# A matmul over 64 rows of the array, done over all 128 rows with zeros

## The chip, the cores and the metric

The kernel runs on one core of one Trainium2 chip. The metric is the device time of one execution in microseconds. A time given for a kernel is the median of several runs.

The core has five engines that the profile names: PE (TensorE, matmuls; PEld is its loading of weights, which overlaps), DVE (VectorE), ACT (ScalarE), POOL (GpSimd) and SP (SyncE, which issues the transfers). Each executes its own instructions in order. They wait for each other at semaphores.

## The reference

Two stages follow each other: an attention of eight batches and eight heads with a feature map, and a feed-forward layer on its output ("MoE" in the code's names, with one expert).

```python
def phi(x):                               # x: batch, head, 576 tokens, 64
    proj = x @ w_phi                      # 64 -> 128 features
    proj = proj - max(abs(proj), last axis)
    return concat([exp(proj), exp(-proj)])  # 256 features
q_p, k_p = phi(q), phi(k)
kv  = einsum('bhsf,bhsd->bhfd', k_p, v)
z   = sum of k_p over tokens
out = (q_p @ kv) / (q_p @ z + 1e-6)

h = x @ w_in                              # 4608 tokens, 512 -> 2048
y = max(0.01 * h, h) @ w_out              # 2048 -> 512
```

The change is in the product of `k_p` and `v`.

## The kernel before

**Numbers.** Most matmuls run on float32r operands. A factor that needs more precision is split into a high part (the value rounded to float32r) and a remainder (value minus high part). A product is then three matmuls: high by high, remainder by high, high by remainder, all added up in the same PSUM tile. In the attention, `vh` and `vl` are the high part and remainder of the values, `kph` and `kpl` those of the features of the keys. `vh` has two extra columns of ones, so that the sum `z` comes out of the same matmul, and so it has 66 columns where `vl` has 64.

**Work.** The attention goes over 32 pairs of heads (4 pairs by 8 batches). For each pair there is a key phase (`k_phase`) and a query phase (`q_phase`). The first eight pairs run their key phase on plain float32, without the split (the branch `nat`, and `first_k_phase` for the first four); the other 24 use the split. The feed-forward layer goes over 18 blocks of 256 tokens and 16 groups of 128 hidden units: `layer1` (lines 542, 543 and 545 issue its matmuls, ACT applies the activation, and the result is split into `gh` and `gl`) and, three steps later, `layer2` (lines 562 to 564).

**A key phase.** A pair of heads has 576 tokens, taken in chunks of 128 on the partitions. Four chunks (c = 0 to 3) hold the first 512 tokens. For each chunk and head (j = 0, 1) the two-part features meet the two-part values in three matmuls over 128 rows. The fifth chunk (c = 4) holds tokens 448 to 575, of which only the last 64 are new. They lie on partitions 64 to 127 (the slice `r`). Their high part goes to the upper half of the tile `kst` by a cast on DVE (recorded at line 69), and their remainder to its lower half, partitions 0 to 63, by a subtraction on DVE (line 264). `kst` appears as `kph` in the profile, after the buffer that it shares. The values of these tokens are loaded twice, into both halves of columns 8 and 9 of `rv`, so `vh[:, 8 + j]` holds them in both halves. One matmul over 128 rows then gives high by high and high by remainder together. What is left is remainder of values by high part of features: a matmul over the 64 upper rows alone, `vl[r, 8 + j]` by `kst[r, j]`. The helper `kv_mm` issues all of these, so they have line 206. In 24 key phases there are 48 of the 64-row matmuls. `vl` is one tile for the whole program, written for each pair by POOL (recorded at line 72); columns 8 and 9 of it are written and read on partitions 64 to 127 alone.

**Order.** The work is written as generators. A key phase and a query phase advance in turn, attention is advanced beside the feed-forward steps, and priorities are given. A scheduler with a model of the engines' time then fixes each engine's order before the program runs. So an edit in one place can move instructions in many. On the chip each engine follows this order.

Of the kernel before, what the change touches and what calls it, by code (L numbers as in the profile page):

```python
# [9 lines left out]
F32 = mybir.dt.float32  # L10
# [34 lines left out]
def attention_moe_kernel(ctx: ExitStack, tc: tile.TileContext, q, k, v, vt, w_phi, w_in, w_out, out):  # L45
    nc = tc.nc
# [4 lines left out]
    def ct(shape, dt, name):  # L51
        return cp.tile(shape, dt, tag=name, name=name)

    def st(shape, dt, tag):
        return sp.tile(shape, dt, tag=tag, name=tag, bufs=BUFS.get(tag, 1))
# [8 lines left out]
    def copy_(key, o, i):  # L64
        e = pick(key) or "a"
        if e == "a":
            nc.scalar.copy(o, i)  # L67
        else:
            (nc.vector if e == "v" else nc.gpsimd).tensor_copy(o, i)  # L69

    def tt_(key, o, a, b, op):
        (nc.vector if pick(key) == "v" else nc.gpsimd).tensor_tensor(o, a, b, op=op)  # L72

    def pt(tag):
        return ps.tile([P, 512], F32, tag=tag, name=tag, bufs=PBUFS[tag])
# [19 lines left out]
    vh = ct([P, 10, 66], F32R, "vh")  # L95
    vl = ct([P, 10, 64], F32R, "vl")
    nc.gpsimd.memset(vh[:, :, 64:66].bitcast(F32), 1.0)

    f1, f2, f3, f4 = (cp.tile([P, 2048], F32, tag="late", name=n, bufs=4) for n in ("f1", "f2", "f3", "f4"))
    fk = [None, f2, f1, f4]  # L100
# [87 lines left out]
    def k_phase(i):  # L188
# [16 lines left out]
        def kv_mm(j, lt, rt, first=False, last=False):  # L205
            nc.tensor.matmul(kvp[0 : lt.shape[1], 256 * j : 256 * j + 256], lhsT=lt, rhs=rt,  # L206
                             start=first and j == 0, stop=last, skip_group_check=True)

        for g in range(3):
            w = 2 if g < 2 else 1  # L210
            r = slice(0, P) if g < 2 else slice(64, P)
            n = P if g < 2 else 64
            m4 = st([P, 4], F32, "m4")
            pmk = st([P, 4, F], F32, "pmk")
            if nat:
                pk = pt("a")
                for s in range(w):
                    t0 = (2 * g + s) * P if g < 2 else S - P
                    proj(pk, s, rk[:, t0 : t0 + P])
                pkv = pk[r, 0 : 256 * w].rearrange("p (a f) -> p a f", f=F)  # L220
            else:
                for s in range(w):
                    t0 = (2 * g + s) * P if g < 2 else S - P
                    pk = pt("a")
                    for j in range(2):
                        nc.tensor.matmul(pk[:, 256 * j : 256 * j + 256], lhsT=ks[:, j, t0 : t0 + P],
                                         rhs=wq.rearrange("p a f -> p (a f)"), start=True, stop=True)
                    pk = pk[r].rearrange("p (j x f) -> p j x f", j=2, x=2)
                    x = pmk[r, 2 * s : 2 * s + 2]
                    copy_("pk", x, pk[:, :, 1])  # L230
                    nc.vector.tensor_tensor(x, pk[:, :, 0], x, op=ALU.add)
                    yield
                pkv = pmk[r, 0 : 2 * w]
            nc.vector.tensor_reduce(m4[r, 0 : 2 * w], pkv, axis=AX.X, op=ALU.max, apply_absolute_value=True)
            mb = m4[r, 0 : 2 * w].unsqueeze(2).broadcast_to([n, 2 * w, F])
            if nat:
                nc.vector.tensor_tensor(pmk[r, 0 : 2 * w], pkv, mb, op=ALU.subtract)
            else:
                tt_("ksub", pkv, pkv, mb, ALU.subtract)
            yield  # L240
            for s in range(w):
                c = 2 * g + s
                ek = st([P, 2, 256], F32, ("ek", "kph", "kpl")[c % 3] if nat else "ek")
                nc.scalar.activation(ek[r, :, 0:F], pmk[r, 2 * s : 2 * s + 2], AF.Exp)  # L244
                nc.scalar.activation(ek[r, :, F:256], pmk[r, 2 * s : 2 * s + 2], AF.Exp, scale=-1.0)
                if nat:
                    for j in range(2):
                        kv_mm(j, rv[r, 4 * j + c if c < 4 else 8 + j], ek[r, j], first=c == 0, last=c == 4)
                    yield
                    continue  # L250
                if c < 4:
                    kph = st([P, 2, 256], F32R, "kph")
                    kpl = st([P, 2, 256], F32R, "kpl")
                    copy_("kph", kph, ek)
                    tt_("kpl", kpl, ek, kph.bitcast(F32), ALU.subtract)
                    for j in range(2):
                        kv_mm(j, vh[:, 4 * j + c], kph[:, j], first=c == 0)
                        kv_mm(j, vl[:, 4 * j + c], kph[:, j])
                    for j in range(2):
                        kv_mm(j, vh[:, 4 * j + c], kpl[:, j])  # L260
                else:
                    kst = st([P, 2, 256], F32R, "kph")
                    copy_("kst", kst[r], ek[r])
                    nc.vector.tensor_tensor(kst[0:64], ek[r], kst[r].bitcast(F32), op=ALU.subtract)
                    for j in range(2):
                        kv_mm(j, vl[r, 8 + j], kst[r, j])
                        kv_mm(j, vh[:, 8 + j], kst[:, j], last=True)
                yield
        kvs = st([P, 2, 256], F32, "ek").rearrange("p a (b f) -> p a b f", b=2)[0:66]
# [107 lines left out]
    def proj(pk, s, x):  # L377
        nc.tensor.matmul(pk[:, 256 * s : 256 * s + 256], lhsT=x, rhs=bd, start=True, stop=True)
# [132 lines left out]
    def attention():  # L511
        for i in range(NP, B * NP + 1):
            gens = [k_phase(i)] if i < B * NP else []
            if i > NP:
                gens.append(q_phase(i - 1))
            while gens:
                for it in list(gens):
                    if next(it, end) is end:
                        gens.remove(it)
                    else:  # L520
                        yield i - 1
            yield i
# [127 lines left out]
```

## Time and profile before

| | |
|---|---|
| median of 3 runs | 1243.11 us (1240.61 to 1243.74) |
| the profiled execution, whole | 1238.5 us |
| its span, first to last instruction | 1236.7 us |
| PE busy in the span | 1187.8 us, 96% |
| DVE busy | 854.6 us, 69% |
| ACT busy | 797.0 us, 64% |
| POOL busy | 669.4 us, 54% |
| TensorE clock granted, mean | 0.994 of full speed |

The profile is of one execution. "PE busy" is the time in which at least one matmul is under way. Matmuls overlap: the next may start well before the last one's recorded end. A group of instructions is shown by line, engine, operation and tile as `out<-in`. Forms such as `64*64 64x256` stand for rows and columns of weights, then partitions and elements of the moving operand. After the bar come busy time and mean duration of one, then idle time of the engine before them and what ended it. Split key phases run from about 230 us to 1045 us; what follows is feed-forward work alone.

### The profile page before, as it was taken

What the parts mean: (1) busy time and instruction counts of PE and PEld (TensorE: products, weight loads), DVE (VectorE), ACT (ScalarE), POOL (GpSimd) and SP (SyncE); (2) the same over time, 40 slices, a digit from 0 to 9 for tenths busy, and PEclk for the clock granted to TensorE, in tenths of its full rate; (3) what the DMA queues carried; (4) which work ended last, traced back from release to release, by engine and by line L of the source; (5) the groups of instructions that cost most, each with busy time, mean ns of one, the idle gap of its engine ahead of it and who ended that gap; (6) DMA issues with size and microseconds to landing.
All of it is one profiled execution on the core that took longest, in us unless ns stands there. A gap on an engine that the chain in (4) does not pass through costs nothing. (4 is left out here: it accounts for less than half of the span.)

```text
span 1236.7 us, 21143 instructions
## 1 busy us (share of the span) xinstructions
PE 1187.8 (96%) x7496; PEld 1035.8 (84%) x7496; DVE 854.6 (69%) x1357; ACT 797.0 (64%) x2027; POOL 669.4 (54%) x701
## 2 busy tenths in 40 slices
PE   8898799999999999999899999999999999999998
PEld 5686577779888989889798988989888888999997
DVE  6999854698888888888888898806887788200000
ACT  5987765677777777777677777736766766433232
POOL 0132122467767676767667777836666767433232
PEclk9999899999999999999999999999999999999999
DMA  7345411011111111111111111100111100000000
GB/s 209 116 135 160 147 47 41 10 54 34 39 30 48 31 35 44 31 48 31 30 38 39 31 48 31 39 20 28 31 48 31 29 20 1 19 17 1 18 18 17
DMA packets 62777, 57.00 MB, mean 46 GB/s; under 512 B 45136, under 2 KB 46288, under 8 KB 62672
## 3 DMA queue, kind: packets, MB, share of 16 engines
q1 hardware_dynamic: 62672, 55.65, 15.8%
q8 instruction: 59, 0.97, 0.3%
q14 instruction: 46, 0.38, 0.1%
HBM read 46.20 MB, written 9.44 MB: 45 GB/s over the span
## 5 line engine op out<-in xcount | busy, mean ns | idle before, releaser
L72 POOL TENSOR_TENSOR gl<-g,gh 128x256 fp32r<-128x256 f32 x288 | 241.9, 842 | 294.8 <-ACT gh L67 237.1
L542 PE MATMUL h<-xh,w0h 128*128 128x256 f32 x1152 | 299.1, 286 | 4.5 <-ACT g L549 1.8
L543 PE MATMUL h<-xh,w0l 128*128 128x256 f32 x1152 | 298.2, 285 | 0.4 <-DVE w0l L72 0.4
L562 PE MATMUL acc<-w1h,gh 128*128 128x512 f32 x576 | 231.0, 401 | 10.4 <-ACT gh L67 8.3
L542 PEld LDWEIGHTS h<-xh,w0h 128*128 128x128 f32 x1152 | 218.4, 190 | 21.2 <-ACT g L549 2.7
L543 PEld LDWEIGHTS h<-xh,w0l 128*128 128x128 f32 x1152 | 218.2, 189 | 14.3 <-issue 1.9
L563 PE MATMUL acc<-w1l,gh 128*128 128x512 f32 x576 | 228.5, 397 | 0.0
L564 PE MATMUL acc<-w1h,gl 128*128 128x512 f32 x576 | 220.3, 398 | 0.0
L545 PE MATMUL h<-xl,w0h 128*128 128x256 f32 x1152 | 206.3, 284 | 0.0
L549 ACT ACTIVATE g<-h 128x256 f32<-128x256 f32 x288 | 109.2, 382 | 133.3 <-PE h L545 93.6
L72 POOL TENSOR_TENSOR ql<-eq,qh 128x576 fp32r<-128x576 f32 x96 | 159.5, 1668 | 38.7 <-DVE qh L69 26.3
L545 PEld LDWEIGHTS h<-xl,w0h 128*128 128x128 f32 x1152 | 167.2, 190 | 2.1 <-issue 0.4
L67 ACT CAST gh<-g 128x256 fp32r<-128x256 f32 x288 | 114.3, 402 | 75.5 <-PE acc L563 72.3
L562 PEld LDWEIGHTS acc<-w1h,gh 128*128 128x128 f32 x576 | 109.0, 189 | 26.3 <-ACT gh L67 10.5
L72 POOL TENSOR_TENSOR kpl<-ek,kph 128x512 fp32r<-128x512 f32 x72 | 101.9, 1415 | 49.9 <-PE c L206 22.1
L69 DVE CAST qh<-eq 128x576 fp32r<-128x576 f32 x96 | 99.2, 1037 | 35.5 <-ACT eq L344 20.1
L564 PEld LDWEIGHTS acc<-w1h,gl 128*128 128x128 f32 x576 | 106.6, 189 | 19.5 <-POOL gl L72 0.5
L563 PEld LDWEIGHTS acc<-w1l,gh 128*128 128x128 f32 x576 | 109.1, 189 | 12.4
L69 DVE COPY o<-acc 128x512 f32<-128x512 f32 x17 | 11.7, 687 | 130.4 <-DMA out_dram<-o 129.5
L72 POOL TENSOR_TENSOR ring<-ring,mb 128x576 f32<-128x576 f32 (+1 forms) x37 | 47.9, 1293 | 88.2 <-DVE mb L500 42.9
L343 ACT ACTIVATE eq<-mb 128x288 f32<-128x288 f32 x112 | 49.3, 440 | 67.8 <-DVE mb L338 60.4
L244 ACT ACTIVATE ek<-pmk 128x256 f32<-128x256 f32 (+1 forms) x128 | 53.4, 417 | 58.6 <-POOL pmk L72 21.0
(176 smaller groups left out, 2412.3 us busy)
## 6 DMA issues: line engine op xcount, KB each, us to landing
out_dram<-o SPq DMA_DIRECT2D x35, 256.0 KB, 2.0
ring<-in_w_in_dram SPq DMA_DIRECT2D x16, 512.0 KB, 3.7
ring<-in_w_out_dram SPq DMA_DIRECT2D x16, 512.0 KB, 3.6
rk<-in_k_dram SPq DMA_DIRECT2D x27, 288.0 KB, 2.8
rq<-in_q_dram SPq DMA_DIRECT2D x26, 288.0 KB, 2.8
rv<-in_v_dram SPq DMA_DIRECT2D x29, 256.0 KB, 3.4
rv<-in_vt_dram SPq DMA_DIRECT2D x58, 32.0 KB, 2.9
f<-in_k_dram SPq DMA_DIRECT2D x3, 288.0 KB, 3.3
```

The costliest lines, as they stand in the source:

```text
L67: nc.scalar.copy(o, i)
L69: (nc.vector if e == "v" else nc.gpsimd).tensor_copy(o, i)
L72: (nc.vector if pick(key) == "v" else nc.gpsimd).tensor_tensor(o, a, b, op=op)
L244: nc.scalar.activation(ek[r, :, 0:F], pmk[r, 2 * s : 2 * s + 2], AF.Exp)
L343: nc.scalar.activation(eq[:, 0], mb[:, u], AF.Exp)
L542: nc.tensor.matmul(ph, lhsT=weight(0, "h", ft)[:, d * P : d * P + P], rhs=xh[:, d], start=d == 0, stop=False)
L543: nc.tensor.matmul(ph, lhsT=weight(0, "l", ft)[:, d * P : d * P + P], rhs=xh[:, d], start=False, stop=False)
L545: nc.tensor.matmul(ph, lhsT=weight(0, "h", ft)[:, d * P : d * P + P], rhs=xl[:, d], start=False, stop=d == NP - 1)
L549: nc.scalar.activation(g, ph, AF.Prelu, alpha=0.01)
L562: nc.tensor.matmul(a, lhsT=gh[:, ts], rhs=weight(1, "h", ft), start=ft == 0, stop=False)
L563: nc.tensor.matmul(a, lhsT=gh[:, ts], rhs=weight(1, "l", ft), start=False, stop=False)
L564: nc.tensor.matmul(a, lhsT=gl[:, ts], rhs=weight(1, "h", ft), start=False, stop=ft == NFT - 1)
```

## The change

The matmul of the values' remainders for the last 64 tokens now takes all 128 rows of both operands. The lower half of its left operand, `vl[0:64, 8:10]`, is set to zero once at the start by POOL, so the product is the same: the lower rows add zero times the features' remainders. The moving operand is now the whole of `kst[:, j]`, both halves.

```diff
     vh = ct([P, 10, 66], F32R, "vh")
     vl = ct([P, 10, 64], F32R, "vl")
     nc.gpsimd.memset(vh[:, :, 64:66].bitcast(F32), 1.0)
+    nc.gpsimd.memset(vl[0:64, 8:10].bitcast(F32), 0.0)
...
                     copy_("kst", kst[r], ek[r])
                     nc.vector.tensor_tensor(kst[0:64], ek[r], kst[r].bitcast(F32), op=ALU.subtract)
                     for j in range(2):
-                        kv_mm(j, vl[r, 8 + j], kst[r, j])
+                        kv_mm(j, vl[:, 8 + j], kst[:, j])
                         kv_mm(j, vh[:, 8 + j], kst[:, j], last=True)
```

All line numbers above 97 are one higher in the changed kernel, so its line 207 is line 206 of before.

The scheduler's order changes with it. On PE, in the first split key phase, at the matmuls of the last 64 tokens (`kph` is the tile `kst`; `qs` and `wq` belong to a query phase, `ks` to the next pair's keys), before:

```order
L226 MATMUL a<-wq,ks 128x256 [waits DVE_49]
L206 MATMUL c<-kph,vl 64x256 [waits DVE_49]
L319 MATMUL a<-qs,wq 128x288 [waits PE_49,Activation_49]
L320 MATMUL a<-qs,wq 128x288
L206 MATMUL c<-kph,vh 66x256 [waits DVE_49]
L206 MATMUL c<-kph,vl 64x256
L206 MATMUL c<-kph,vh 66x256
```

and now:

```order
L227 MATMUL a<-wq,ks 128x256 [waits DVE_49]
L320 MATMUL a<-qs,wq 128x288 [waits PE_49,Activation_49]
L321 MATMUL a<-qs,wq 128x288
L207 MATMUL c<-kph,vl 64x256 [waits DVE_49]
L207 MATMUL c<-kph,vh 66x256
L207 MATMUL c<-kph,vl 64x256
L207 MATMUL c<-kph,vh 66x256
```

The size behind the tiles is that of the output, so the 64 there is columns of `vl` in both. The first `vl` matmul has moved behind the query's two, next to its `vh`, and one wait for DVE stands where two stood.

The same place on PE in the second split key phase, where the work between is layer 1's, before:

```order
L543 MATMUL h<-xh,w0l_798 128x256
L206 MATMUL c<-kph,vl 64x256 [waits DVE_49]
L542 MATMUL h<-xh,w0h_797 128x256
L543 MATMUL h<-xh,w0l_798 128x256
L542 MATMUL h<-xh,w0h_797 128x256
L543 MATMUL h<-xh,w0l_798 128x256
L542 MATMUL h<-xh,w0h_797 128x256
L206 MATMUL c<-kph,vh 66x256 [waits DVE_49]
L206 MATMUL c<-kph,vl 64x256
L206 MATMUL c<-kph,vh 66x256
```

and now:

```order
L543 MATMUL h<-xh,w0h_798 128x256
L544 MATMUL h<-xh,w0l_799 128x256
L543 MATMUL h<-xh,w0h_798 128x256
L544 MATMUL h<-xh,w0l_799 128x256
L207 MATMUL c<-kph,vl 64x256 [waits DVE_49]
L207 MATMUL c<-kph,vh 66x256
L207 MATMUL c<-kph,vl 64x256
L207 MATMUL c<-kph,vh 66x256
```

The first `vl` matmul stands six places later, behind more of layer 1, and the four are together.

On POOL, at the start of the program, now:

```order
L128 MEMSET bd 128x256
L125 MEMSET rv 128x10x2
L125 MEMSET f_79 128x10x2
masks.py:197 MEMSET ident 128x128
L97 MEMSET vh 128x10x2
L98 MEMSET vl 64x128
masks.py:199 ISA
masks.py:199 AFFINE_SELECT ident<-ident 128x128
```

The new memset of `vl` stands behind those of `bd`, which holds `w_phi`, and of the first tiles; the other rows stand as before.

## The prediction

> **What bounds the kernel now.** I read the page's engine table and slices first, then a table by stage, then the groups by form, the timeline around the changed matmul, the waits, and last the chain.
>
> ```profile
> span 1236.7 us, 21143 instructions
> PE 1187.8 (96%) x7496; PEld 1035.8 (84%) x7496; DVE 854.6 (69%) x1357; ACT 797.0 (64%) x2027; POOL 669.4 (54%) x701
> PE   8898799999999999999899999999999999999998
> DVE  6999854698888888888888898806887788200000
> PEclk9999899999999999999999999999999999999999
> ```
>
> TensorE is busy nearly all the time, at nearly full clock, so the clock is no term of the sum. DVE stands at 8 to 9 tenths while attention runs and is the second limit there. The stage table (stretch, length, then busy time and count of PE, PEld, DVE, ACT, POOL) gives the margin in the stage where the changed matmuls lie, and in a piece of it that the chain below covers.
>
> ```profile
> 230.00:1050.00 820.00, 797.72 (x5277) 712.56 (x5275) 669.16 (x1015) 573.89 (x1495) 559.64 (x546) 1.00 0.12 34
> 971.00:1045.00 74.00, 71.19 (x470) 62.72 (x469) 60.04 (x92) 53.17 (x141) 52.84 (x54) 1.00 0.06 17
> ```
>
> TensorE is idle for 820 - 797.72 = 22.3 us there (2.7%), and for 74 - 71.19 = 2.8 us (3.8%) in the piece. DVE is busy 669.16 of 820, or 82%. So the stage runs at the pace of TensorE, with some points at which TensorE has to wait.
>
> But a busy TensorE need not be a TensorE at its peak. Overlapped matmuls count as busy even where they are spaced out. What a matmul costs the stream is the time from its start to the next one's start. The groups by form hint at it:
>
> ```profile
> L206 PE MATMUL c<-kph,vl 128*64 128x256 f32 x192 | 49.5, 280 | 0.0
> L206 PE MATMUL c<-kph,vl 64*64 64x256 f32 x48 | 15.7, 328 | 0.7 <-DVE kph L69 0.7
> L206 PEld LDWEIGHTS c<-kph,vl 64*64 64x64 f32 x48 | 6.2, 129 | 10.4 <-issue 5.4 <-DVE kph L69 1.6 <-DVE kph L264 0.6
> ```
>
> The first row is the same product on 128 rows (of the first 512 tokens), the second the 64-row form that the change replaces: 48 of them, two in each of 24 phases. They are only 48 ns longer each, which alone would be 2.3 us. The third row tells more: the weight loads of this form have 10.4 us of idle time before them, most of it "issue", that is, waiting for nothing that the profile shows.
>
> **The timeline shows the real price.** First the normal case, the 128-row form between its neighbours (start, duration):
>
> ```profile
> 229.85 0.28 PE L206 MATMUL c<-kph,vh 128*66 128x256 f32 x1
> 229.97 0.28 PE L206 MATMUL c<-kph,vl 128*64 128x256 f32 x1
> 230.09 0.28 PE L206 MATMUL c<-kph,vh 128*66 128x256 f32 x1
> 230.20 0.28 PE L206 MATMUL c<-kph,vl 128*64 128x256 f32 x1
> 230.32 0.39 PE L563 MATMUL acc<-w1l,gh 128*128 128x512 f32 x1
> ```
>
> Four matmuls in 230.32 - 229.85 = 0.47 us: 0.117 us from start to start, though each lasts 0.28. Each starts while the one before is still under way. Now the 64-row form, between 128-row ones, with no wait for any engine:
>
> ```profile
> 281.88 0.28 PE L542 MATMUL h<-xh,w0h 128*128 128x256 f32 x1
> 282.00 0.27 PE L206 MATMUL c<-kph,vh 128*66 128x256 f32 x1
> 282.20 0.33 PE L206 MATMUL c<-kph,vl 64*64 64x256 f32 x1
> 282.46 0.34 PE L206 MATMUL c<-kph,vh 128*66 128x256 f32 x1
> 282.63 0.40 PE L226 MATMUL a<-wq,ks 128*128 128x256 f32 x2
> ...
> 311.20 0.63 PE L545 MATMUL h<-xl,w0h 128*128 128x256 f32 x4
> 311.76 0.33 PE L206 MATMUL c<-kph,vl 64*64 64x256 f32 x1
> 312.01 0.50 PE L562 MATMUL acc<-w1h,gh 128*128 128x512 f32 x1
> 312.35 0.40 PE L563 MATMUL acc<-w1l,gh 128*128 128x512 f32 x1
> 312.59 0.40 PE L226 MATMUL a<-wq,ks 128*128 128x256 f32 x2
> ```
>
> In the first piece the starts lie 0.20, 0.26 and 0.17 us apart, 0.63 us in all, where three normal steps make 3 x 0.117 = 0.35. The 64-row matmul costs the stream 0.28 us beyond its own step. In the second piece the last of the four L545 starts at about 311.20 + 3 x 0.117 = 311.55, and the steps are 0.21, 0.25 and 0.34. Normal would be 0.117, 0.117 and, after a 512-column matmul, 0.24 (312.35 to 312.59). The excess is 0.80 - 0.47 = 0.33 us. Here the matmul behind has 128 columns of weights to load, in the first piece 66. So the stream empties before a 64-row matmul and again behind it, and the next weights are not loaded ahead.
>
> **What the change removes.** The second matmul of each phase's pair is always followed by the 66-column vh (0.28 us). The first of the pair is followed by that or by other work (up to 0.33 us). I take 24 x 0.28 + 24 x 0.33 = 14.6 us for the 48. The row of the 128-row form says what stays in their place: the normal step, already taken off. The bounds are 48 x 0.28 = 13.4 and 48 x 0.33 = 15.8 us.
>
> Against it speaks a rule of the Trainium skill (TensorE: Matmul & The Clock Gate, section "Why this matters for your kernels"): one matmul of few rows takes the same time as one of 128, and only running several side by side gains. By it the sum would be zero, and the time 1243.1 us. The rows above disagree for this stream. The skill itself names a reason (TensorEngine Tiling, section "Key Properties"): a change of tiling mode drains TensorE. It gives no figure.
>
> **How much of it reaches the end.** Where DVE or ACT set the pace, a faster TensorE only waits longer. The chain of waits (start, length, what) shows the last such stretch:
>
> ```profile
> 970.99 0.51 ACT kph L67
> 975.89 0.79 DVE mb L369
> 997.33 1.59 DVE qh L69
> 998.96 0.40 PE a L358
> 1043.71 0.64 PE c L206 x3
> ```
>
> From about 971 to 999 us the chain runs over DVE and ACT, and from there to the end of attention over TensorE. That is 28 of 74 us, 38%, in a stretch with 3.8% of idle TensorE. Before 969 us this view follows no further. I scale by TensorE's idle share: 38% x 2.7 / 3.8 = 27% of the stage, an estimate. So about 27% of the gain, 3.9 us, is swallowed, and 14.6 - 3.9 = 10.7 us remain. The ends are nothing swallowed (14.6) and, if DVE holds everywhere, all of it (0).
>
> **What the change adds.** The matmul now also reads the lower half of kst, which DVE writes last, in the subtraction of L264. Before, the first vl matmul of a phase waited only for the cast. These are the two instructions (minimum, median, maximum) and TensorE's waits for them (total, times, longest):
>
> ```profile
> L264 DVE TENSOR_TENSOR kph<-ek,kph x24: 685/687/1710, 248.2 to 1041.8; 64x512 fp32r<-64x512 f32 x24
> L69 DVE CAST kph<-ek x24: 423/425/1016, 247.8 to 1040.8; 64x512 fp32r<-64x512 f32 x24
> PE c L206 <- DVE kph L69: 0.7, 2, 0.4
> PE c L206 <- DVE kph L264: 0.5, 1, 0.5
> PE a L358 <- DVE qh L69: 8.3, 10, 1.4
> ```
>
> In the new order the four matmuls stand together where the vh stood, which already waited for L264, and the work that lay between them now stands ahead. So two waits become one at the later place. That lost 0.5 us once in 24 phases and 0.7 us in two. I take zero. Below, the 0.7 us of the earlier wait may go. Above, L264's 0.69 us may fall on TensorE in each phase, 24 x 0.69 = 16.5 us. Zero is nearest to the rows. Queued behind the waiting matmul is all of TensorE's in-order stream, with the MoE matmuls for which ACT and POOL wait.
>
> The regenerated order also shifts MoE matmuls ahead of attention's (the first vl in the second piece shown stands six places later). This gives DVE about 6 x 0.117 = 0.7 us more before TensorE needs it, and could shorten the 8.3 us that TensorE waits for qh. In turn DVE may wait longer for TensorE, which was
>
> ```profile
> DVE tq L321 <- PE a L320: 8.8, 14, 1.4
> ```
>
> I take zero for both together. For the range I allow 4 us either way, about half of these 8 us.
>
> The zeros themselves cost one POOL memset of 64x128 at the start:
>
> ```profile
> 1.07 0.20 POOL masks.py:197 MEMSET ident<- 128x128 f32 x1
> 22.00 0.12 POOL L178 MEMSET rv<- 128x20 f32 x1 [20.24 <-PE h L413]
> ```
>
> At most 0.2 us, by the ident row, behind the memset of bd that the first load waits for. POOL then stands idle for 20 us. Without that cover it would still be 0.2 us, once. The lower half of vl is written by nothing else, so it is not done again.
>
> **The sum.** 14.6 - 3.9 + 0 + 0 = 10.7 us less. The profiled execution took 1238.5 us (span 1236.7 and 1.8 around it), so it would be 1227.8. That execution lay 4.6 us under the median of the runs; carried to the median, 1243.1 - 10.7 = 1232.4 us. No change can be told within 0.3%, or 3.7 us: faster begins below 1239.4.
>
> **The rivals.**
>
> All of it arrives. TensorE is 97% busy in the stage, so it may be the pace nearly everywhere, and the new order may shorten waits: 1243.1 - 14.6 = 1228.5, down to 1224 with 4 us of shorter waits. Against it stand the 28 us of chain off TensorE.
>
> DVE takes over. DVE's 82% and its in-order chain through ACT's exponentials become the pace. At 65% or more swallowed, 14.6 x 0.35 = 5.1 us or less remains: 1238 to 1243. Against it, half of the shown piece's chain and more runs over TensorE, in a stretch with more waits than the mean.
>
> The joined wait costs (the other side). If TensorE reaches the four matmuls before L264 is done in most phases, it stands still there. With L264's median in each phase 24 x 0.69 = 16.5 us is added, net 16.5 - 10.7 = 5.8 us slower, 1248.9. With its longest, 1.71 us, in a quarter of them it is 24 x (0.75 x 0.69 + 0.25 x 1.71) = 22.7, net 12 us, 1255. It decides from 10.7 / 24 = 0.45 us a phase. Against it: the wait on L264 at this place cost 0.5 us in all.
>
> No drain is removed, because the spacing comes from the output's 64 columns or from switching tiles: 1243.1. Against it, the 128*64 rows above have the same columns and normal steps.
>
> **The numbers.** Forecast (8 to 12.5 us less) 0.58; all of it 0.20; DVE takes over 0.13; the joined wait 0.06; no drain removed, the skill's equal-time rule with it, 0.03. The forecast and the full gain are faster, and of DVE's case a third: 0.82 faster. The rest of it, the last case and some of the joined wait's are within: 0.13. Slower 0.05. The range runs from 1224 (full gain and 4 us of waits) to 1240 (DVE takes over, mostly).
>
> **What would show it.** The form 64*64 of vl is gone, its 48 join the 128*64 row at about 280 ns, and the steps around them are 0.12 us. PE's busy time in the span falls by about as much as the span. TensorE's idle time between 230 and 1050 grows by some 4 us if DVE swallows as said. A wait "PE c L206 <- DVE" of over 5 us would show the joined wait. The forecast is wrong if the steps stay wide, if TensorE's waits grow by over 10 us, or if they shrink by more than 5.

## The result and the profile after

The changed kernel takes 1232.01 us (median of 4 runs, 1230.23 to 1233.99), the one before, run beside it, 1242.97 (1240.61 to 1243.74). The ratio is 0.9915, with a 95% interval of 0.9891 to 0.994: 10.5 us less, between 7 and 14. Forecast was 1232.4. The number was met; the experiments show that its terms were not.

First what came as said. The group of the 64-row form is gone from the groups by form on PE, and its 48 stand in the 128-row row:

```profile
L207 PE MATMUL c<-kph,vh 128*66 128x256 f32 x240 | 61.9, 280 | 3.4 <-ACT kph L67 3.2
L207 PE MATMUL c<-kph,vl 128*64 128x256 f32 x240 | 61.8, 280 | 0.0
```

The timeline of PE in the changed kernel, at a group for the last 64 tokens, has the normal step:

```profile
314.34 0.40 PE L227 MATMUL a<-wq,ks 128*128 128x256 f32 x2
314.57 0.28 PE L207 MATMUL c<-kph,vl 128*64 128x256 f32 x1
314.69 0.28 PE L207 MATMUL c<-kph,vh 128*66 128x256 f32 x1
314.81 0.28 PE L207 MATMUL c<-kph,vl 128*64 128x256 f32 x1
314.93 0.28 PE L207 MATMUL c<-kph,vh 128*66 128x256 f32 x1
315.04 0.40 PE L563 MATMUL acc<-w1h,gh 128*128 128x512 f32 x1
```

Four matmuls in 0.47 us, 0.12 each. Nothing is left of the steps of 0.20 to 0.34.

What did not come as said is in the engine table, the stage table and the waits of the changed kernel:

```profile
span 1232.2 us, 21145 instructions
PE 1176.2 (95%) x7496; PEld 1037.0 (84%) x7496; DVE 849.2 (69%) x1357; ACT 794.5 (64%) x2027; POOL 670.1 (54%) x702
PEclk9999989999999999999899999999999999999999
...
230.00:1050.00 820.00, 792.91 (x5326) 720.53 (x5325) 668.52 (x1023) 576.24 (x1506) 563.44 (x551) 0.99 0.12 34
594.40:601.20 6.80, 5.88 (x26) 5.87 (x27) 5.39 (x8) 5.26 (x15) 5.87 (x5) 0.50 0.10 39
601.20:608.00 6.80, 6.80 (x47) 6.21 (x46) 6.02 (x6) 5.63 (x15) 4.99 (x5) 1.00 0.25 82
...
PE a L359 <- DVE qh L69: 9.7, 15, 1.1
PE h L543 <- ACT g L550: 3.3, 2, 2.9
PE c L207 <- ACT kph L67: 3.2, 3, 1.9
```

TensorE's idle time from 230 to 1050 us has risen from 22.3 to 820 - 792.91 = 27.1 us. One new wait, 2.9 us for ACT's activation, stands at 592 us. Around its end a stretch of 6.8 us at half clock begins: 26 matmuls in that stretch, 47 in the next of the same length. (Both belong to the new order and not to the rows, as a run with 64 rows in this order shows below.) This profiled execution took 1234.0 us, at the slow end of its kernel's runs, and that of before 1238.5, at the fast end of its own, so the two traces differ by only 4.5 us. The comparisons below go by ratios of several runs to the kernel before on the same chip; 0.001 of it is 1.24 us.

### The profile page after: what moved, and what is told of

Same layout as the page of the kernel before. It is cut to its first block, busy times and chain, and to the rows that moved or that the text cites. A ratio compares the mean times of both kernels' runs of the same rounds, so it can differ in the third digit from the quotient of the medians.

```text
span 1232.2 us, 21145 instructions
## 1 busy us (share of the span) xinstructions
PE 1176.2 (95%) x7496; PEld 1037.0 (84%) x7496; DVE 849.2 (69%) x1357; ACT 794.5 (64%) x2027; POOL 670.1 (54%) x702
## 5 line engine op out<-in xcount | busy, mean ns | idle before, releaser
L546 PE MATMUL h<-xl,w0h 128*128 128x256 f32 x1152 | 200.8, 283 | 0.0
L69 DVE CAST qh<-eq 128x576 fp32r<-128x576 f32 x96 | 96.3, 1006 | 37.2 <-ACT eq L345 17.4
```

The lines of the kernel that those rows point to most:

```text
L546: nc.tensor.matmul(ph, lhsT=weight(0, "h", ft)[:, d * P : d * P + P], rhs=xl[:, d], start=False, stop=d == NP - 1)
```

## Experiments

### The price on TensorE by itself

```diff
-            nc.tensor.matmul(a, lhsT=gl[:, ts], rhs=weight(1, "h", ft), ...)
+            rr = slice(64, P) if i >= NBLK - 3 else slice(0, P)
+            nc.tensor.matmul(a, lhsT=gl[rr, ts], rhs=weight(1, "h", ft)[rr], ...)
```

> The changed kernel, with the 96 matmuls L565 (gl by w1h, 512 columns) of the last three blocks on their upper 64 rows alone (so half of the remainder product there is not computed). They stand behind the end of attention, where TensorE alone sets the pace and nothing is swallowed. Theory: each costs the stream about 0.33 us more than a 128-row one, 96 x 0.33 = 32 us, 1264. Rival (a matmul of few rows takes the same time and costs its stream nothing): 1232.

Every engine's order is that of the changed kernel. Measured: 1264.73 us, ratio 1.0188 (1.0168 to 1.0208). Against the changed kernel's 0.9915 that is 0.0273, or 34 us for 96 matmuls, 0.35 us each. The timeline there:

```profile
1180.84 0.39 PE L564 MATMUL acc<-w1l,gh 128*128 128x512 f32 x1
1181.15 0.50 PE L566 MATMUL acc<-w1h,gl 64*128 64x512 f32 x1
1181.58 0.50 PE L563 MATMUL acc<-w1h,gh 128*128 128x512 f32 x1
1181.91 0.40 PE L564 MATMUL acc<-w1l,gh 128*128 128x512 f32 x1
```

The steps are 0.31, 0.43 and 0.33 where 0.23 is normal: 0.38 us in excess. So a 64-row matmul among 128-row ones does cost its stream 0.3 us and more, although it multiplies half as much, and where TensorE alone sets the pace all of it reaches the end. This price is shown.

### The new order without the rows

The first two runs keep 64 rows and only issue the four matmuls in another sequence. The scheduler then makes another order of the whole.

```diff
                     for j in range(2):
                         kv_mm(j, vl[r, 8 + j], kst[r, j])
+                    for j in range(2):
                         kv_mm(j, vh[:, 8 + j], kst[:, j], last=True)
```

> The kernel before, with the two 64-row matmuls of a phase issued one behind the other (both vl, then both vh). The work is the same. Theory (the stream empties at each change between 64 and 128 rows): each pair now has one change in and one out, where it had two of each, so 24 x 0.31 = 7.3 us of the 14.6 us go away on TensorE; with 27% swallowed by DVE, 5.3 us less than before, 1237.7. The step between the two 64-row matmuls of a pair should be about 0.12 us, the step into the pair about 0.20 and out of it about 0.26. Rival (each 64-row matmul is slow by itself): steps as before, 1243. Rival (new order alone made the gain): 1243, give or take 4.

Measured: 0.9988 (0.9977 to 0.9998), 1.5 us less, not 5.3. In its timeline the pair steps as the theory says, but the time did not follow:

```profile
282.24 0.28 PE L544 MATMUL h<-xh,w0l 128*128 128x256 f32 x1
282.45 0.44 PE L206 MATMUL c<-kph,vl 64*64 64x256 f32 x2
282.82 0.39 PE L543 MATMUL h<-xh,w0h 128*128 128x256 f32 x1
283.04 0.28 PE L544 MATMUL h<-xh,w0l 128*128 128x256 f32 x1
```

From 282.24 to 283.04 are four steps in 0.80 us where four normal ones make 0.47: 0.33 us for two 64-row matmuls together, as much as a single one costs. So TensorE pays for each change of rows and not for each matmul. That only a fifth of the 7.3 us arrived was a first sign that more is swallowed than I had said, though the order is another one too.

```diff
-                        kv_mm(j, vl[r, 8 + j], kst[r, j])
-                        kv_mm(j, vh[:, 8 + j], kst[:, j], last=True)
+                        kv_mm(j, vh[:, 8 + j], kst[:, j])
+                        kv_mm(j, vl[r, 8 + j], kst[r, j], last=True)
```

> The kernel before, with 64 rows, but each vh issued ahead of its vl, so that vl stands behind the one wait for L264, as in the changed kernel, and the four matmuls stand together. This is the joined wait and the later place without the 128 rows. Theory: the 48 x 0.30 us stay, so the time is that of before, 1243, give or take the 4 us allowed for a new order. Rival (the gain comes from the joined wait and the new order): 1232, as the changed kernel. Rival (the joined wait costs, hidden under the gain): 1248 or more, with waits of c L206 for DVE of over 5 us.

Measured: 1.0002 (0.999 to 1.0014). The joined wait and this new order together change nothing; a gain and a loss that cancel are not excluded. It is not the changed kernel's order, though, and that is the weakness of this run.

### The rows alone, the order held

A dependency of the 64-row matmul on the subtraction makes the scheduler take the changed kernel's order, row for row and wait for wait on every engine. `after_` adds that dependency.

```diff
-                    nc.vector.tensor_tensor(kst[0:64], ek[r], ...)
+                    low = nc.vector.tensor_tensor(kst[0:64], ek[r], ...)
                     for j in range(2):
-                        kv_mm(j, vl[:, 8 + j], kst[:, j])
+                        mm = kv_mm(j, vl[r, 8 + j], kst[r, j])
+                        after_(mm, low)
                         kv_mm(j, vh[:, 8 + j], kst[:, j], last=True)
```

> The changed kernel, its matmuls back on 64 rows, with a dependency on the subtraction L264 added, so that the order and the waits of every engine are those of the changed kernel row for row. Only the rows differ. Theory: the 48 emptyings are back, 14.6 us on TensorE, of which about 10.7 reach the end: 1243, as before. If the new order had helped by itself, it would lie between: the difference to the changed kernel is the price of the rows alone, whatever the order did. Rival (order and joined wait made the gain): 1232.

The changed kernel ran beside it:

> The changed kernel once more, on the same chip as the next three, so that they can be set against it. 1232, 0.9915 of before, in the interval measured so far.

Measured: 64 rows in the new order 0.9962 (0.9948 to 0.9977), the changed kernel 0.9926 (0.9914 to 0.9939). Neither my theory (1.000) nor the rival (0.992) has it. The new order alone gives 0.0038, 4.7 us (2.9 to 6.5). The rows alone give 0.0036, 4.5 us, with an uncertainty of 2.5 (the two intervals' half-widths, 0.0013 and 0.0015, combined). Yet on TensorE the whole price is back. The timeline of this run at the same group as shown above of the changed kernel:

```profile
313.08 0.40 PE L231 MATMUL a<-wq,ks 128*128 128x256 f32 x2
313.41 0.33 PE L211 MATMUL c<-kph,vl 64*64 64x256 f32 x1
313.66 0.33 PE L211 MATMUL c<-kph,vh 128*66 128x256 f32 x1
313.93 0.33 PE L211 MATMUL c<-kph,vl 64*64 64x256 f32 x1
314.18 0.33 PE L211 MATMUL c<-kph,vh 128*66 128x256 f32 x1
314.35 0.39 PE L568 MATMUL acc<-w1h,gh 128*128 128x512 f32 x1
```

From the second L231 (313.20) to L568 it is 1.15 us; in the changed kernel, from 314.46 to 315.04, 0.58. That is 0.57 us a phase, 24 x 0.57 = 13.7 us in all, near the forecast's 14.6. Summed step by step around all 48 matmuls, the two traces differ by 13.7 us too. So 13.7 us leave TensorE's stream and about 4.5 reach the end: two thirds are swallowed, and with the uncertainty of 2.5 between a half and 85%, not 27%.

The two traces show where a part of it goes. These rows are of the run with 64 rows:

```profile
230.00:1050.00 820.00, 796.51 (x5275) 714.27 (x5275) 664.34 (x1014) 573.16 (x1497) 559.12 (x546) 0.99 0.12 34
595.00:601.80 6.80, 6.17 (x27) 6.16 (x28) 5.39 (x8) 5.26 (x14) 6.16 (x5) 0.50 0.10 39
...
PE h L548 <- ACT g L555: 3.1, 2, 2.7
```

TensorE is idle for 820 - 796.51 = 23.5 us, where the changed kernel has 27.1. So 3.6 us of the gain turn into waits. The long wait for ACT (2.7 us) and the half clock behind it are here as well, so they are not what swallows the gain in this pair. The rest is not found in the traces: this execution took 1239.3 us, the longest of six, and the spans of the two traces, 1237.5 and 1232.2, differ by 5.3 us. The span of a second trace of the changed kernel is 1228.8. The two thirds rest on the medians of several runs.

The pair of 64-row matmuls side by side, within this order:

```diff
                     for j in range(2):
                         mm = kv_mm(j, vl[r, 8 + j], kst[r, j])
                         after_(mm, low)
+                    for j in range(2):
                         kv_mm(j, vh[:, 8 + j], kst[:, j], last=True)
```

> The 64-row kernel with the changed kernel's order, but within each phase vl, vl, vh, vh in place of vl, vh, vl, vh; every other row of the order is the same. The first such pairing, in the kernel before, won only 1.6 us and also got another order and two more stretches of half clock. Theory (price per change of rows, order the same now): 7.3 us less on TensorE than with vl, vh, vl, vh, of which 73% to all arrive: 5.3 to 7.3 us less than the run with the rows alone put back. Rival (price per 64-row matmul): no difference to that run.

Measured: 0.9948 (0.9936 to 0.9961), 0.0014 or 1.7 us below the run with vl, vh, vl, vh, with an uncertainty of 2.4. The theory's 5.3 to 7.3 is out, since it took too little as swallowed; no difference at all is inside, and so is a third of the 7 us, which would be 2.3. The time decides nothing between these two. The timeline does, with one price for the pair (from 312.04, the second L231, to 312.91 it is 0.87 us where five normal steps make 0.59):

```profile
311.92 0.40 PE L231 MATMUL a<-wq,ks 128*128 128x256 f32 x2
312.25 0.44 PE L211 MATMUL c<-kph,vl 64*64 64x256 f32 x2
312.62 0.45 PE L211 MATMUL c<-kph,vh 128*66 128x256 f32 x2
312.91 0.39 PE L569 MATMUL acc<-w1h,gh 128*128 128x512 f32 x1
```

A second pair of runs that differ in the rows alone is the one with vh ahead of vl (`vl` has its zeros as in the changed kernel):

```diff
                         kv_mm(j, vh[:, 8 + j], kst[:, j])
-                        kv_mm(j, vl[r, 8 + j], kst[r, j], last=True)
+                        kv_mm(j, vl[:, 8 + j], kst[:, j], last=True)
```

> The order of e2_late (vh ahead of vl), now with 128 rows: every engine's order is that of e2_late but for the memset on POOL. A second pair that differs in the rows alone. Theory: 10.7 us less than e2_late's 1241.7, 1231. If part of the gain of the changed kernel came from its order: less than 8 us.

Measured: 0.9995 (0.9986 to 1.0004) against 1.0002 with 64 rows. In this order the rows are worth 0.9 us, with an uncertainty of 1.9: next to nothing. Here are the stage rows of the two, first 64 rows and then 128, and two stretches of the second at half clock:

```profile
230.00:1050.00 820.00, 797.81 (x5271) 712.97 (x5272) 662.15 (x1008) 574.92 (x1495) 559.22 (x547) 1.00 0.12 34
```

```profile
230.00:1050.00 820.00, 790.04 (x5270) 716.13 (x5270) 660.87 (x1007) 573.01 (x1496) 559.64 (x546) 0.99 0.12 34
599.70:606.50 6.80, 6.10 (x27) 6.10 (x28) 6.50 (x7) 4.62 (x14) 5.46 (x6) 0.50 0.10 39
804.50:807.90 3.40, 3.40 (x17) 3.22 (x16) 2.59 (x3) 3.25 (x7) 3.40 (x4) 0.50 0.00 1
```

Summed around the 48 matmuls, 14.9 us left TensorE's steps. Its idle time rose by 797.81 - 790.04 = 7.8 us, and these two stretches of half clock, which the 64-row run does not have, cost half of TensorE's busy time in them, (6.10 + 3.40) / 2 = 4.7 us. Together that is 12.5 of the 14.9. So in these two executions most of the gain went into waits and into half clock. The second execution has the lowest clock of its kernel's eleven runs, 0.987; the means over the runs of the two kernels are 0.991 and 0.989, which is 2 us rather than 4.7.

### Is DVE what swallows it?

I expected DVE to be the second limit. So I took work off DVE, with every instruction held at its place in the changed kernel's order, once with 64 rows and once with 128.

```diff
+            tn = tj if nat else tj[:, 0:1]
-            nc.vector.tensor_tensor(tj, tj, m[:, j]..., op=ALU.subtract)
+            nc.vector.tensor_tensor(tn, tn, m[:, j, 0 : tn.shape[1]]..., op=ALU.subtract)
```

> The 64-row kernel with the changed kernel's order (as e6_rows, the order now held by dependencies), and less work on DVE: the 48 subtractions of the features' bound in the split query phases (0.94 us each) act on 32 of 576 columns, so that part of the query features is not computed as in the reference. This takes some 48 x 0.7 = 34 us off DVE and nothing off TensorE; no instruction changes its place. It is one half of a pair with the next run. If DVE is what swallows TensorE's gain, TensorE's waits for DVE shrink and this run is some 10 us or more below e6_rows' 1236.

> The changed kernel with the same 34 us taken off DVE and its order held. Theory (DVE's pace swallows the gain of the rows: at full DVE work 128 rows were worth only 4.3 us of the 14 on TensorE): with DVE relieved they are worth 10 to 14.6 us against the run before. Rival (the gain is lost elsewhere, to ACT, POOL or the clock): 4 us, as at full DVE work.

Measured: 0.9811 (0.9798 to 0.9825) with 64 rows and 0.9776 (0.9762 to 0.9791) with 128. Taking the subtractions off DVE gives 0.015, 19 us, in both. But the rows are still worth only 0.0035, 4.3 us (uncertainty 2.5), just as at full DVE work. My theory fell; the rival had the number. The relief was smaller than the 34 us that I had estimated, though: DVE's busy time fell from 850.5 to 828.6 us with 64 rows and from 849.2 to 832.1 with 128, and DVE stays 68% busy or more. The waits of TensorE in the stage, for 64 rows and then for 128:

```profile
PE a L370 <- DVE qh L74: 2.9, 5, 0.7
PE h L554 <- ACT g L561: 0.6, 2, 0.3
...
230.00:1050.00 820.00, 809.26 (x5404) 729.99 (x5402) 651.67 (x1027) 583.11 (x1523) 565.31 (x557) 1.00 0.12 35
```

```profile
PE a L365 <- DVE qh L74: 4.6, 9, 1.0
PE h L549 <- ACT g L556: 2.1, 2, 1.8
...
230.00:1050.00 820.00, 803.85 (x5431) 735.15 (x5430) 655.76 (x1028) 584.30 (x1529) 567.85 (x558) 0.99 0.12 35
```

The idle time is 16.2 us with 128 rows where the changed kernel has 27.1, and it still rose by 809.26 - 803.85 = 5.4 us when the rows changed, a part of it behind DVE's casts, a part behind ACT. So DVE's load costs the kernel time, but the one job of DVE that was lightened here is not what swallows the gain; DVE's other jobs were not tried. My reading is that in a fixed order TensorE meets the other engines' results at many points with little time to spare, and that what it saves between two such points is waited for at the next. Idle time that rises in all three pairs, by 3.6, 7.8 and 5.4 us, fits it. Which engine holds each point was not settled.

### The rows without the new order

The changed kernel's work, held in the order of the kernel before: the first vl of a phase stays early, and waits there for L264.

> 128 rows in the order of the kernel before, row for row (held by dependencies): the first vl of a phase stays at its early place, and there it now waits for L264. It shows the change without its new order. Theory (the rows are worth some 4 us where DVE swallows the rest, and an early wait costs TensorE up to 0.69 us in each of 24 phases): 1236 if the wait finds L264 done, 1236 + 16 = 1252 if it never does; I expect 1240, with c L206's waits for DVE up by a few us. Rival (no part of the new order): 1232, as the changed kernel.

Measured: 0.9969 (0.9958 to 0.998), 3.9 us less than before; I expected 1240, 3 less. The wait of this run that I had expected:

```profile
PE c L212 <- DVE kph L270: 9.8, 10, 2.8
```

L270 is the subtraction of L264. At the old place TensorE waits 9.8 us for it, in ten phases, where the kernel before waited 0.5. The changed kernel has no such wait at all: the scheduler, which knew of the dependency, put the four matmuls where it was met. So the new order is worth 0.9969 - 0.9926 = 0.0043, some 5 us, at 128 rows, and a similar 4.7 at 64. The two are not the same thing: at 128 rows the new order also does away with this wait, which at 64 rows is all but absent (0.5 us). The 128 rows are worth 3.9 us in the old order, with the new wait already taken off, and 4.5 in the new one.

### Less work on TensorE

```diff
                     for j in range(2):
-                        kv_mm(j, vl[:, 8 + j], kst[:, j])
                         kv_mm(j, vh[:, 8 + j], kst[:, j], last=True)
```

> The changed kernel with the 48 vl matmuls of the last 64 tokens left out (so a part of the remainder product is not computed). It takes another 48 x 0.117 = 5.6 us off TensorE and nothing off the other engines. Theory (27% swallowed by DVE): 4.1 us less than the changed kernel, 1227.9. If nothing is swallowed: 1226.4. If DVE is the pace by now: 1232. A new order may move each by 4.

Measured: 1218.37 us, 0.9815 (0.9795 to 0.9835), 12 to 14 us below the changed kernel and far outside all three expectations. The work left out is 5.6 us. The rest goes with the order, which the scheduler made anew. Its idle time from 230 to 1050 us is 20.0 us where the changed kernel has 27.1:

```profile
230.00:1050.00 820.00, 799.96 (x5368) 725.96 (x5367) 660.27 (x1028) 585.49 (x1527) 570.08 (x557) 1.00 0.12 35
```

So the run could not tell what it was made for. It suggests that another order of nearly the same work can be worth 7 to 8 us, more than the rows or the new order here; work and order changed together, so this is argued and not shown.

### A version that beats both

```diff
-                    nc.tensor.matmul(pq, lhsT=bd[r, F * j : F * j + F], rhs=rq[r, us], start=True, stop=True)
+                    nc.tensor.matmul(pq, lhsT=bd[:, F * j : F * j + F], rhs=rq[:, us], start=True, stop=True)
```

> The changed kernel, with the 32 other 64-row matmuls of the plain-float32 query phases (L318) on all 128 rows too: their left operand has zeros outside its block already, so both operands are only taken whole. The order is the changed kernel's. In its trace an isolated pair of these costs the stream 0.39 us beyond its steps, in 8 phases of 32 matmuls, at most 16 stops: 6.2 us on TensorE. If nothing is swallowed: 1225.8; with 70% swallowed, as the rows alone showed: 1230.1. Faster than both kernels in either case. A 128-row one would cost it more if it had run beside its neighbour on the other half of the array, as one pair in the trace does (starts 7 ns apart): then up to 2 us is given back.

Measured: 1228.43 us, 0.9892 (0.9876 to 0.9907), 4.2 us below the changed kernel (uncertainty 2.5), in its order. I had given 6.2 us less if nothing is swallowed and 1.9 less with 70% swallowed; the uncertainty holds both. This is the fastest version here that leaves no work out. The same step, zeros in place of half the rows, was already paid for: `bd` is block-diagonal.

## Why the prediction was right, and where it was wrong

**The price on TensorE: right.** Step "what the change removes": 14.6 us. With the order held it measured 13.7, and 0.35 us for each matmul in the stretch where nothing hides it. The rule of the Trainium skill that I had weighed against it (TensorE: Matmul & The Clock Gate, "Why this matters for your kernels": one matmul of few rows takes the same time as one of 128) does not hold for this stream. The other (TensorEngine Tiling, "Key Properties": a change of mode drains TensorE) agrees with the runs; the price that it leaves out is about 0.3 us for a way in and out.

**How much reaches the end: wrong.** I took 27% as swallowed, from one stretch of the chain scaled by TensorE's idle share. Measured with the order held it is about two thirds (4.5 of 13.7 arrive, uncertainty 2.5), and in another order nearly all (0.9 of 14.9, uncertainty 1.9). The chain shows what set the pace with the stops in place. It does not show the paths that lie just behind it; that these take over as soon as the stops are gone is my reading and was not shown path by path. The rival "DVE takes over", 65% or more swallowed, which had 0.13, describes this term better than my forecast, though its time, 1238 to 1243, did not come. DVE as the only cause was not borne out. What neither the rival nor I had is the clock: with vh ahead of vl, two further stretches at half clock came with the 128 rows in the execution shown.

**The joined wait and the new order: wrong by one term.** I set both to zero, with 4 us of play. The new order gives some 5 us. Held at the old place the wait costs 9.8 us in ten phases, so the rival's mechanism exists; in the changed kernel it does not occur, as I had argued from the place of vh, and the price is zero as said.

**The sum.** Forecast: 14.6 - 3.9 + 0 = 10.7. Measured: about 4.5 from the rows and 4.7 from the order, 9.2 in that comparison, 10.5 in the first. Two errors, about 6 us too much in the one term and about 5 too little in the other, cancelled. That the number was met is luck. "All of it arrives" and "no drain is removed" are refuted. The sign that I had named for the swallowing, 4 us more idle time from 230 to 1050, came (4.8), and I would have read it as a confirmation; it does belong to the rows in the main (3.6 of the 4.8), but only the run with the order held showed that it stood beside a gain of another origin.

**Open:** which engine holds TensorE at each of its waits, where the swallowed part beyond the 3.6 us of waits goes, and what in the order gave the 4.7 us: it stands in the medians, and the kept traces do not show it (1236.7 us before, 1237.5 with 64 rows in the new order). About 1 us on TensorE could be the 64-row matmuls of a phase standing closer together (13.7 us where I counted 14.6 for them apart); that was not tried by itself.

## What to carry to other kernels

Read the steps from start to start, not durations: here a matmul on 64 rows among matmuls on 128 costs its stream about 0.3 us on the way in and out, so fill it up with zeros, or put such matmuls side by side so that they share one way in and out (shown in the steps, within the noise in the time). Where a scheduler sets the order, hold the order before crediting an edit with a change of time; here the rows and the order each made about half. A chain of waits says what held the pace before the change; the waits that come next are not in it, and here they took more than it let expect.

## What the runs showed of the hardware

The half clock was not in my sum. In the changed kernel's timeline, behind the wait at 592 us, the steps between matmuls are nearly twice as long:

```profile
595.32 0.58 PE L543 MATMUL h<-xh,w0h 128*128 128x256 f32 x1 [2.92 <-ACT g L550]
595.69 0.42 PE L544 MATMUL h<-xh,w0l 128*128 128x256 f32 x1
595.91 0.41 PE L543 MATMUL h<-xh,w0h 128*128 128x256 f32 x1
...
601.28 0.28 PE L543 MATMUL h<-xh,w0h 128*128 128x256 f32 x1
601.40 0.28 PE L544 MATMUL h<-xh,w0l 128*128 128x256 f32 x1
```

They are 0.22 us until 601 and 0.12 from there. The wait cost 2.9 us, and the 5.88 us in which TensorE is busy at half clock about another 2.9. A second execution of the changed kernel shows the same wait (first row), then stretches at half clock; the last row is of the first execution again:

```profile
593.00 0.39 PE L543 MATMUL h<-xh,w0h 128*128 128x256 f32 x1 [2.91 <-ACT g L550]
...
594.20:597.60 3.40, 3.40 (x18) 3.39 (x17) 2.44 (x4) 2.48 (x7) 3.40 (x4) 0.51 0.21 77
723.90:727.30 3.40, 3.40 (x11) 2.73 (x10) 3.40 (x4) 1.42 (x5) 3.01 (x4) 0.50 0.01 2
...
725.90:729.30 3.40, 3.38 (x20) 3.04 (x21) 3.10 (x5) 2.03 (x7) 2.97 (x3) 1.00 0.00 0
```

Behind the same wait the half clock lasts 6.8 us in one execution and 3.4 in the other, where it begins 1.2 us after the wait's end. A wait of 1.9 us for ACT ends at 725.9 us in the first execution and at 722.5 in the second; half clock came behind it in the second alone. So the length of a wait alone does not decide it. The stretches shown here are 3.4 or 6.8 us long. The Trainium skill (TensorE: Matmul & The Clock Gate, section "What's actually happening") tells of a free-running window of 3413 ns by whose activity the clock is set, and these lengths agree with it. Such a window would also give a reason why the same wait has different consequences: it may fall into one window or across two. That reason was argued and not tried. It does not explain why runs of one kernel differ by 3 us: of these two executions the one with the lower mean clock (0.990 against 0.992) is the shorter, 1228.8 against 1232.2 us.
